# The last three output stores are issued from ScalarE's queue instead of SyncE's

## The chip, the cores and the metric

The kernel runs on one core of one Trainium2 chip. The metric is the device time of one execution in microseconds. Before the change it is 194.41 us, the median of three runs (194.31 to 195.1 us). One further execution was profiled; it took 194.51 us. Engines are named as the profile names them: PE is TensorE (PEld its weight loads), DVE is VectorE, ACT is ScalarE, POOL is GpSimd, SP is SyncE, which computes nothing and issues DMAs. A name with a q behind it (SPq, ACTq) is the sequencer of that engine, the part that takes the instructions in order, waits for semaphores and issues DMAs.

## The reference

A gated linear attention for 4 batches and 8 heads, followed by a block with a short causal convolution as a gate, and two matrix products:

```python
for t in range(S):                       # S = 768, per batch and head, D = 48
    state = f[:, :, t, :, None] * state + k[:, :, t] (x) v[:, :, t]
    y[:, :, t] = q[:, :, t] @ state
x = y as (B, S, 384)
gate = sigmoid(sum over 5 taps of conv_w[k] * x shifted by k)
out = (gate * (x @ w_val)) @ w_out
```

Here f is the sigmoid of f_logit, and (x) is an outer product.

## The kernel before

The 768 steps are cut into six chunks of 128. For each chunk the attention part makes the rows of x in SBUF, and the output part turns them into the result. The output part works on units: the tuples of UNITS say which chunk and which batches a unit holds. Chunks 1 to 4 are one unit each; the first and the last chunk are cut into two halves of two batches. The units of the last chunk are number 6 and number 7, and number 7 runs first. A unit has three column blocks of 128 (m or o is 0, 1, 2).

The order of all work is written out by hand in the string PROGRAM (line 54): every entry such as "mout 6 2" is a piece of the kernel with its unit and its block, and the loop on line 846 calls them in that order. The class Ordered ties each engine's instructions to the order in which they are recorded; since all are recorded through its one line, almost all instructions stand under line 129 in the profile, and one goes by the tiles' names.

For each block of a unit, "mout" runs nine matmuls on PE into a PSUM bank (bk), and "mstore" copies that bank into SBUF on ACT and then starts the DMA to the output from SP. Each DMA waits for the copy's semaphore. The program ends with:

```python
mout 7 2; mrest 6 1; mhigh 6 2; mmul 6 0; mrest 6 2; mhigh 6 0; mout 7 1; mstore 7 2; mrest 6 0; mout 6 2;
mstore 7 1; mout 6 1; mstore 6 2; mout 6 0; mstore 6 1; mstore 6 0
```

The six stores of the last chunk use six buffers in turn: ca, cb, ca, cb, osb, osb (four buffers that served the weights, and two that served earlier stores). In the order of the stores, the last three are block 2 of unit 6 out of the second cb, block 1 out of the first osb and block 0 out of the second osb. Each is 128 x 256 numbers, 128 KB. In store() (line 811), the list with the name ends counts these six.

DMAs use eight semaphores in turn. The store before the last three, the one of the second ca, has the first of them, the last three have the second, third and fourth.

Behind the last piece every engine does the same: it loads a flag (line 850, in the profile TENSOR_LOAD of bad) that says whether the inputs need a general path, and branches past that path (line 852, COMPARE_BRANCH). With these inputs all engines branch past it. On the far side each engine waits for its own unfinished work (line 852, EVENT_SEMAPHORE); SP has eight such waits, one for each DMA semaphore, in the order of the semaphores, so the last store is its fourth. Then SP has eight more on line 904 (the end of the program), and all engines meet in a closing barrier, also on line 904. SP loads the flag earlier than the others, ahead of its last twelve stores, so what it does behind its last DMA begins with the branch.

Of the kernel before, what the change touches and what calls it, by code (L numbers as in the profile page):

```python
# [140 lines left out]
def gla_moe(ctx: ExitStack, tc: tile.TileContext, q, k, f, v, wv, cw, wo, ft, out):  # L141
# [7 lines left out]
    PE, DVE, ACT, SP, POOL = (Ordered(tc, e) for e in (nc.tensor, nc.vector, nc.scalar, nc.sync, nc.gpsimd))  # L149
# [48 lines left out]
    def give(*key):  # L198
        free.append(held.pop(key))
# [359 lines left out]
    def mstart(xf, b0, b1, **t):  # L559
        return {"xf": xf, "b": slice(b0, b1), "n": (b1 - b0) * C, **t}  # L560
# [64 lines left out]
        w["po", o] = bank  # L625
        mm3(w["po", o][:, : w["n"]], lambda kk: woH[:, kk], lambda kk: woL[:, kk], w, "gH", "gL", o)

    def mstore(w, o, buf, dst):
        ACT.copy(buf, w["po", o][:, : w["n"]])
        SP.dma_start(dst, buf)  # L630

    def oview(c, o, b0=0, b1=B):
        return out[c, :, o, b0:b1].rearrange("p b t -> p (b t)")


    def general(ctx):
# [66 lines left out]
        with tc.For_i(0, NC, 1) as c:  # L703
            xf = gp.tile([128, NM, B, HALO + C], F32, name="gxf")
            for m in range(NM):
                for to, at, n in turned(m):
                    nc.sync.dma_start(xf[to : to + n, m], X[m * 128 + at : m * 128 + at + n, :, bass.ds(c * C, HALO + C)])
            w = mstart(xf, 0, B, **{n: gp.tile([128, NM, B, C], F32 if n == "gt" else F32R, name="g" + n)[:]
                                    for n in ("xH", "xL", "gt", "gH", "gL")})
            msplit(w)  # L710
            mlow(w)
            vps = [gb.tile([128, 1024], F32, name="vps") for _ in range(2)]
            for m in range(NM):
                w["gp", m] = vps[m // 2][:, m % 2 * 512 : m % 2 * 512 + 512]
            for j in range(KT):
                mconv(w, j)
            for m in range(NM):
                mgate(w, m)
            for m in range(NM):
                mval(w, m, gb.tile([128, 1024], F32, name="vps"))  # L720
                mmul(w, m)
                mhigh(w, m)
                mrest(w, m)
            for o in range(NM):
                mout(w, o, gb.tile([128, 1024], F32, name="vps"))
                mstore(w, o, g2.tile([128, B * C], F32, name="gosb")[:], out[bass.ds(c, 1), :, o].rearrange("u p b t -> (u p) (b t)"))
# [6 lines left out]
    proj, late, stored, ends = {}, {}, [], []  # L733

    def retag(tag, n, dtype=F32R):

        if tag not in late:
            late[tag] = mp.tile([128, n], dtype, name="r" + tag, tag=tag)
        return late[tag]

    def view(n):
        if n not in proj:
            c, b0, b1 = UNITS[n]
            at = (b0 // 2) * N2
            x = (dict(zip(("xH", "xL", "gt"), (t[:, :, b0:b1] for t in (xH, xL, gt)))) if c < last else

                 {"xH": part(retag("e2", 2 * N2), at, 2), "xL": part(retag(f"e1{(last - 2) % NE}", 2 * N2), at, 2)})
            proj[n] = mstart(XF[c % 2], b0, b1, turned=c >= CS, **x)
        return proj[n]
# [61 lines left out]
    def store(n, m):  # L811
        c, b0, b1 = UNITS[n]
        if c < last:
            buf = osb[len(stored) % len(osb)][:, : view(n)["n"]]
            stored.append(n)
        else:
            bufs = [t for ab in cab for t in ab] + osb
            buf = bufs[len(ends) % len(bufs)][:, : view(n)["n"]]
            ends.append(n)
        mstore(view(n), m, buf, oview(c, m, b0, b1))  # L820
        give("mout", n, m)

    def mul(n, m):
# [18 lines left out]
        "mval": lambda n, m: mval(view(n), m, take("mval", n, m)), "mmul": mul,  # L842
        "mhigh": lambda n, m: mhigh(gated(n), m), "mrest": lambda n, m: mrest(gated(n), m),
        "mout": lambda n, m: mout(gated(n), m, take("mout", n, m)), "mstore": store,
    }
    for piece in PROGRAM.replace("\n", " ").split(";"):
# [62 lines left out]
```

## Time and profile before

| what | value |
| --- | --- |
| median of three runs | 194.41 us |
| the profiled execution | 194.51 us |
| its span, from first to last instruction | 192.8 us |
| outside the span in that execution | 1.7 us |
| PE busy | 179.4 us (93%) |
| DVE busy | 161.4 us (84%) |
| ACT busy | 144.6 us (75%) |
| granted TensorE clock | 0.998 |
| DMAs issued by SP | all |

The first part of a page gives the busy time of each engine. DMA-issuing, waiting and branching instructions count as no engine's busy time, and so the chain of waits of the profile ends with the last computing instruction. What comes behind it is seen only in the rows of the sequencers (names with a q), which the views by line and by tile show. In the rows of a DMA issue, "us to landing" runs from the start of the issue to the arrival of the last of its sixteen semaphore increments.

### The profile page before, as it was taken

What the parts mean: (1) busy time and instruction counts of PE and PEld (TensorE: products, weight loads), DVE (VectorE), ACT (ScalarE), POOL (GpSimd) and SP (SyncE); (2) the same over time, 40 slices, a digit from 0 to 9 for tenths busy, and PEclk for the clock granted to TensorE, in tenths of its full rate; (3) what the DMA queues carried; (4) which work ended last, traced back from release to release, by engine and by line L of the source; (5) the groups of instructions that cost most, each with busy time, mean ns of one, the idle gap of its engine ahead of it and who ended that gap; (6) DMA issues with size and microseconds to landing.
All of it is one profiled execution on the core that took longest, in us unless ns stands there. A gap on an engine that the chain in (4) does not pass through costs nothing.

```text
span 192.8 us, 8306 instructions
## 1 busy us (share of the span) xinstructions
PE 179.4 (93%) x3706; PEld 144.3 (75%) x3706; DVE 161.4 (84%) x233; ACT 144.6 (75%) x284; POOL 16.0 (8%) x42
## 2 busy tenths in 40 slices
PE   3999999987999899999999999999999999999970
PEld 1888875675996468888788877878788778978960
DVE  7279899985998979979899998999993899998900
ACT  5899896999789997579999988594555856258530
POOL 6020111231000350000000000000000000000000
PEclk9999999999999999999999999999999999999999
DMA  5999999998647232643922319334000130011231
GB/s 199 331 411 423 418 415 405 409 346 248 191 124 297 15 112 55 212 142 113 341 79 84 112 53 313 84 137 167 3 3 3 58 111 3 3 58 54 86 113 39
DMA packets 12522, 32.64 MB, mean 169 GB/s; under 512 B 3008, under 2 KB 5440, under 8 KB 11456
## 3 DMA queue, kind: packets, MB, share of 16 engines
q1 hardware_dynamic: 12480, 32.04, 46.9%
q8 instruction: 31, 0.51, 1.1%
q14 instruction: 11, 0.09, 0.2%
HBM read 26.51 MB, written 4.72 MB: 162 GB/s over the span
## 4 chain that ended last, share of the span: by engine, by line
PE 59%; DVE 22%; ACT 9%; issue 5%; POOL 0%
PE bk L129 52%; PE aps L129 8%; DVE re L129 7%; DVE gt L129 5%; ACT ss L129 3%; DVE asb L129 2%; ACT xf L129 2%; DVE ca L129 1%; DVE cb L129 1%; DVE xL L129 1%; DVE kb L129 1%; ACT e L129 1%; DVE rg L129 1%; ACT gt L129 1%; DVE qb L129 1%
## 5 line engine op out<-in xcount | busy, mean ns | idle before, releaser
L129 ACT ACTIVATE e<-e 112x512 f32<-112x512 f32 (+4 forms) x38 | 36.7, 997 | 4.2 <-DMA e<-in_ft 2.0
L129 DVE TENSOR_TENSOR asb<-aps,tri 128x768 f32<-128x768 f32 (+1 forms) x24 | 25.0, 1040 | 7.0 <-PE aps L129 5.9
L129 PE MATMUL bk<-rg,woH 128*128 128x512 f32 (+1 forms) x108 | 30.1, 365 | 0.1
L129 DVE SCALAR_TENSOR_TENSOR gt<-xf,cws,gt 128x512 f32<-128x512 f32 x36 | 26.5, 749 | 1.5 <-ACT gt L129 0.9
L129 PEld LDWEIGHTS aps<-qb,kb 48*64 48x64 f32 (+1 forms) x640 | 19.9, 144 | 7.3 <-issue 4.8
L129 PE MATMUL bk<-asb,vb 128*32 128x64 f32 (+2 forms) x1280 | 24.2, 232 | 0.4 <-issue 0.3
L129 PE MATMUL aps<-qb,kb 48*64 48x128 f32 (+2 forms) x640 | 23.7, 257 | 0.1
L129 PEld LDWEIGHTS bk<-asb,vb 128*32 128x32 f32 (+1 forms) x1280 | 19.9, 108 | 4.0 <-issue 1.1
L129 PEld LDWEIGHTS bk<-rg,woH 128*128 128x128 f32 x108 | 18.6, 188 | 4.2 <-issue 0.8
L129 PE MATMUL bk<-rg,woL 128*128 128x512 f32 (+1 forms) x54 | 19.3, 358 | 0.0
L129 DVE TENSOR_TENSOR kb<-kb,e 112x1024 f32<-112x1024 f32 (+1 forms) x13 | 14.8, 1137 | 5.2 <-ACT e L129 5.0
L129 DVE TENSOR_TENSOR_SCAN e<-keep,e 112x1024 f32<-112x1024 bf16 x8 | 18.3, 2282 | 0.0
L129 ACT ACTIVATE ss<-u,e 112x48 f32<-112x48 f32 x64 | 15.3, 322 | 3.3 <-PE bk L129 3.3
L129 PE MATMUL bk<-qb,ss 48*32 48x128 f32 x640 | 15.8, 275 | 1.8 <-ACT cb L129 0.9
L129 ACT COPY osb<-bk 128x512 f32<-128x512 f32 (+1 forms) x20 | 9.8, 494 | 8.3 <-DMA out<-osb 5.1
L129 DVE TENSOR_TENSOR qb<-qb,e 112x1024 f32<-112x1024 f32 (+1 forms) x13 | 15.0, 1160 | 0.0
L129 ACT COPY xf<-bk 128x384 f32<-128x384 f32 x24 | 10.8, 471 | 5.2 <-PE bk L129 5.2
L129 PEld LDWEIGHTS bk<-qb,ss 48*32 48x32 f32 x640 | 10.6, 106 | 4.8 <-issue 3.1
L129 PE MATMUL bk<-xH,wvH 128*128 128x256 f32 (+1 forms) x36 | 13.3, 370 | 0.0
L129 PE MATMUL bk<-xL,wvH 128*128 128x256 f32 (+1 forms) x36 | 12.2, 339 | 0.0
L129 POOL MEMSET mark<- 1x1 f32 x18 | 1.6, 88 | 127.7 <-PE bk L129 127.7
L129 PE MATMUL bk<-xH,wvL 128*128 128x256 f32 (+1 forms) x36 | 12.2, 338 | 0.0
(107 smaller groups left out, 350.9 us busy)
## 6 DMA issues: line engine op xcount, KB each, us to landing
kb<-in_k SPq DMA_DIRECT2D x9, 512.0 KB, 4.5
qb<-in_q SPq DMA_DIRECT2D x9, 512.0 KB, 5.0
e<-in_f SPq DMA_DIRECT2D x4, 1024.0 KB, 10.3
vb<-in_v SPq DMA_DIRECT2D x9, 448.0 KB, 4.4
out<-osb SPq DMA_DIRECT2D x12, 256.0 KB, 2.1
raww<-in_wv SPq DMA_DIRECT2D x1, 1152.0 KB, 9.0
raww<-in_wo SPq DMA_DIRECT2D x1, 1152.0 KB, 11.3
kb<-in_k SPq DMA_DIRECT2D x1, 1024.0 KB, 13.6
```

Of the source, the lines that this page charges most:

```text
L129: ins = emit(*a, **kw)
```

## The change

The function mstore gets the queue that issues the DMA as an argument. store() passes ACT for the fourth to the sixth store of the last chunk, and SP for all others. The copies, buffers, transfers and their order stay.

```diff
-    def mstore(w, o, buf, dst):
+    def mstore(w, o, buf, dst, queue=SP):
         ACT.copy(buf, w["po", o][:, : w["n"]])
-        SP.dma_start(dst, buf)
+        queue.dma_start(dst, buf)
...
             ends.append(n)
-        mstore(view(n), m, buf, oview(c, m, b0, b1))
+
+        mstore(view(n), m, buf, oview(c, m, b0, b1), ACT if len(ends) > 3 else SP)
         give("mout", n, m)
```

One line is added to the file ahead of the end, so lines 850, 852 and 904 become 851, 853 and 905.

On ACT, at the end of the program, in one piece of the difference between the two programs (each row with the semaphores that it waits for; DMAHW are the eight DMA semaphores, PE_49, DVE_49 and Activation_49 those of the engines):

```order
 L129 COPY cb_104<-bk_110 128x256 [waits PE_49]
+L129 DMA out<-cb_104 128x256 [waits Activation_49]
 L129 COPY osb_97<-bk_106 128x256 [waits DMAHW4_49,PE_49]
+L129 DMA out<-osb_97 128x256 [waits Activation_49]
 L129 COPY osb_98<-bk_111 128x256 [waits DMAHW5_49,PE_49]
-L850 TENSOR_LOAD bad [waits DVE_49]
-L852 COMPARE_AND_BRANCH
+L129 DMA out<-osb_98 128x256 [waits Activation_49]
+L851 TENSOR_LOAD bad [waits DVE_49]
+L853 COMPARE_AND_BRANCH
```

Each of ACT's last three copies is now followed by a DMA that waits for that copy, and the flag and the branch come behind the third DMA.

On SP, at the same place:

```order
 L129 DMA out<-cb_102 128x256 [waits DMAHW7_49,Activation_49]
 L129 DMA out<-ca_103 128x256 [waits DMAHW0_49,Activation_49]
-L129 DMA out<-cb_104 128x256 [waits DMAHW1_49,Activation_49]
-L129 DMA out<-osb_97 128x256 [waits DMAHW2_49,Activation_49]
-L129 DMA out<-osb_98 128x256 [waits DMAHW3_49,Activation_49]
-L852 COMPARE_AND_BRANCH
+L853 COMPARE_AND_BRANCH
```

The branch follows directly on the store of ca_103 now. The eight waits behind SP's branch and the eight on the end line are the same in both programs.

## The prediction

> **What bounds the kernel now.** I read the chain of waits first, at its end, since the edit touches only the last stores. It closes like this (start, duration, what):
>
> ```profile
> 183.60 3.35 PE bk L129 x26
> 186.95 0.02 issue
> 186.97 0.37 ACT osb L129
> ```
>
> So PE paces the work up to 186.95 us, and the last computing instruction, the copy behind it, ends at 187.34. The span is 192.84. The windows view, which gives the busy time of PE, PEld, DVE, ACT and POOL, says what stands between the two:
>
> ```profile
> 187.40:192.84 5.44, 0.00 (x0) 0.00 (x0) 0.00 (x0) 0.00 (x0) 0.00 (x0) 0.94 0.15 45
> ```
>
> Nothing computes for 5.44 us. What ends last there is a sequencer. The timeline of the two queues shows the last three copies on ACT, and the last store on SP:
>
> ```profile
> 184.84 0.37 ACT L129 COPY cb<-bk 128x256 f32<-128x256 f32 x1 [1.07 <-PE bk L129]
> 185.91 0.37 ACT L129 COPY osb<-bk 128x256 f32<-128x256 f32 x1 [0.69 <-PE bk L129]
> 186.97 0.37 ACT L129 COPY osb<-bk 128x256 f32<-128x256 f32 x1 [0.69 <-PE bk L129]
> 183.81 0.39 SPq L129 DMA_DIRECT2D out<-ca  x1
> 185.24 0.33 SPq L129 DMA_DIRECT2D out<-cb  x1
> 187.37 0.82 SPq L129 DMA_DIRECT2D out<-osb  x1
> ```
>
> SP issues the last store 0.03 us behind the copy's end and is done with it at 188.19. Then the view of line 852 (the branch past the general path, and the waits behind it), engine by engine, with durations in ns and first and last start:
>
> ```profile
> L852 SPq EVENT_SEMAPHORE  x8: 17/17/17, 190.9 to 191.4; - x8
> L852 SPq COMPARE_BRANCH  x1: 45/45/45, 188.2 to 188.2; - x1
> L852 ACTq COMPARE_BRANCH  x1: 50/50/50, 187.6 to 187.6; - x1
> L852 ACTq EVENT_SEMAPHORE  x1: 17/17/17, 188.0 to 188.0; - x1
> L852 DVEq COMPARE_BRANCH  x1: 72/72/72, 183.7 to 183.7; - x1
> L852 DVEq EVENT_SEMAPHORE  x1: 21/21/21, 186.9 to 186.9; - x1
> L852 PEldq COMPARE_BRANCH  x1: 4138/4138/4138, 185.3 to 185.3; - x1
> L852 PEldq EVENT_SEMAPHORE  x1: 51/51/51, 189.5 to 189.5; - x1
> ```
>
> SP branches at 188.2 and its next instruction starts at 190.9. SP's list of waits books the same time as its own, not as a DMA's:
>
> ```profile
> SPq L852 <- SPq L852: 2.6, 1, 2.6
> ```
>
> DVE loses 3.1 us (183.8 to 186.9) and PE 4.1 us at the same branch, and neither issues DMAs; ACT loses 0.4. So I take SP's 2.6 us as the price of the jump itself, not as a wait for the store. The Trainium skill ("Runtime: NRT & Kernel Launch", section "Instruction fetch mechanics") has a name for it: a taken branch whose target lies outside the fetched window waits for a DMA of code.
>
> Is the store perhaps just as late? Landing times of the last five stores, in the order of issue (183.38, 183.81, 185.24, 186.31, 187.37), from the DMA view of short windows:
>
> ```profile
> out<-cb SPq DMA_DIRECT2D x1, 128.0 KB, 1.7
> out<-ca SPq DMA_DIRECT2D x1, 128.0 KB, 2.7
> out<-cb SPq DMA_DIRECT2D x1, 128.0 KB, 3.8
> out<-osb SPq DMA_DIRECT2D x1, 128.0 KB, 3.1
> out<-osb SPq DMA_DIRECT2D x1, 128.0 KB, 2.8
> ```
>
> The last store lands at 187.37 + 2.8 = 190.2. SP's wait for it is the fourth of its eight, which start evenly from 190.9 to 191.4, 0.07 us apart: at 191.1, about 0.9 us after the landing. **So the branch on SP, begun only behind the last store's issue, sets the end of the kernel; the store is second, 0.9 us behind.** From that fourth wait to the end of the span it is 192.84 - 191.1 = 1.7 us. This stretch holds SP's other four waits, the ones on line 904 and the closing barrier:
>
> ```profile
> L904 SPq EVENT_SEMAPHORE  x10: 17/28/28, 191.5 to 192.7; - x10
> L904 SPq DRAIN  x3: 7/7/7, 192.0 to 192.3; - x3
> ```
>
> SP reaches the barrier at 192.0; the others were there before (PE, the next, at about 189.6).
>
> **The change part by part.** *SP loses three issues.* Its last is now the store of ca, 183.81 + 0.39 = 184.2, and the branch follows. With its own 2.6 us SP is through at 186.8, with PE's 4.1 us at 188.3. Both lie ahead of the last landing, so SP's jump leaves the path, and its waits will stand ready for the last store. Nothing else queues on SP.
>
> *ACT gains three issues.* No row of this trace shows a DMA issued by ACT. The nearest are SP's:
>
> ```profile
> L129 SPq DMA_DIRECT2D out<-osb x20: 332/338/819, 77.5 to 187.4; - x20
> L129 SPq DMA_DIRECT2D wvLt<-wvL x4: 550/594/1390, 47.7 to 50.4; - x4
> ```
>
> Like transfers take 0.34 us as a rule and 0.82 at most; no SP issue of another shape takes over 1.39. I take SP's own values at the same three places, 0.33, 0.33 and 0.82. Queued behind the first two issues are ACT's next copies, each of which waits 0.69 us for PE before it starts; behind the first copy's end (185.21) and the second's start (185.91) there is room for an issue of some 0.6 us. So they cost nothing, hidden under PE's nine matmuls per block; beyond 0.6 us each further 0.1 us is paid twice. PE and DVE wait for no instruction behind these issues. The third store then starts at 187.37, as before.
>
> Behind the third issue ACT still has to load the flag, which stood under its last copy before:
>
> ```profile
> L850 ACTq TENSOR_LOAD <-bad x1: 562/562/562, 187.0 to 187.0; - x1
> ```
>
> That gives 188.2 + 0.56 + 0.05 for the branch + 0.4 for its jump = 189.2, ahead of the landing, and level with PE's 189.5. It costs nothing as long as ACT's jump stays short; if it took SP's 2.6, ACT would be at the barrier at 191.5.
>
> *What is late next: the landing of the third store.* The end of the span becomes landing + 1.7. Bounds for issue to landing are the rows above, 1.7 and 3.8 us: landing from 189.1 to 191.2. By its own row, 2.8, it is 190.2. Between issue and landing SP's code fetch runs in the program of before. Packets of code in two windows of the DMA view, 186.2:186.5 and 189.2:189.4 (packets, MB, share of 16 engines in the window):
>
> ```profile
> q8 instruction: 1, 0.02, 33.4%
> q14 instruction: 1, 0.01, 10.7%
> ```
>
> These are 0.334 x 16 x 0.3 = 1.6 us and 0.107 x 16 x 0.2 = 0.34 us on a DMA engine that stores use too. The first falls in PE's jump, and the stores issued nearest to it (185.24, 186.31) are the ones with the longest landings. The second comes 1.0 us after SP's branch, ahead of the last landing; it moves to about 185.2. An estimate: of its 0.34 us half is saved, so I take the landing at 190.0, between 190.2 and 189.8.
>
> **The sum.** 190.0 + 1.7 = 191.7 for the span, against 192.84: 1.1 us less. The profiled execution would go from 194.51 to 193.4; it stood 0.1 us above the median of the runs, so the forecast is **193.3 us**.
>
> Here a rule weighs in. The Trainium skill ("DMA: Bandwidth & Descriptors", section "Issuing engines are not separate DMA queues") says that issuing from several engines saves no more than sequencer time, since all transfers run on the same 16 engines. Where the trace bears on it, it agrees: the code packets and the stores share engines. By that rule the landing would stay at 190.2 and the sum at 0.9 us less, 193.5.
>
> **The rivals.** *The landing slips (193.6 to 194.4).* SP's code packet, and what it fetches ahead, now run at 185 to 188, beside PE's packet of 1.6 us, when the three stores are in flight. If the last share of the third store lands 0.1 to 0.9 us later than 190.2, only 0.8 to 0 us is left. For it speaks the 3.8 row of the cb store; against it, that the store in question is issued last, at 187.37. ACT's jump at 2.6 us would end alike: 191.5 + 0.8 from SP's 192.0 to the span's end = 192.3, 194.0. It decides from a landing of 190.2, or an arrival of ACT at the barrier after 191.0.
>
> *The third issue's stall goes (192.4).* The 0.82 is 0.48 above the usual. If on ACT's queue it takes 0.34 and lands like the first cb store, in 1.7, the landing is 189.1, the end 190.8, 2.0 us less. For it: a queue of its own with only two stores ahead. Against it: the PE code packet stays where it is.
>
> *A dear issue on ACT (slower, 195.6).* At 1.39 us per issue: first 185.24 to 186.63, copy until about 187.06, second until 188.5, copy until 188.9, third until 190.3. From the end of an issue to the landing it took 2.8 - 0.82 = 2.0 us in the last store: landing 192.3, end 194.0, 1.2 us more. It loses from about 1.0 us per issue; for less the jump's gain covers it. Against it: the median of 338 ns over the twenty osb stores.
>
> *The change does not do what it says:* the order of the instructions shows SP's branch right behind ca, so this is out unless SP's jump also takes until 190.9, 6.7 us; the longest is 4.1.
>
> **How the numbers follow.** About 0.5%, 1.0 us, is what a measurement of this kernel can tell from no change. Forecast case 0.45, 0.03 of it under that line; stall gone 0.15, faster; landing slips or ACT's jump grows 0.33, the same; dear issue 0.07, 0.05 of it slower. That makes faster 0.57, same 0.38, slower 0.05. The bounds of the landing, 189.1 to 191.2, make 192.4 to 194.5; I leave out a thin edge below: 192.5 to 194.5.
>
> **What would show it.** Right: SP's branch on line 853 at 184.2, its first wait after it no later than 188.3, three waits there passing at once and the fourth standing until the landing near 190.0; ACT's issues at 185.24, 186.31 and 187.37, its copies not moved; the closing barrier 1.7 us after the landing. Wrong: ACT issues over 0.6 us, copies that start late, ACT or PE at the barrier behind SP, or a fourth wait that ends past 190.2.

## The result, and the profile after

The changed kernel takes 193.37 us (median of 22 runs, 192.74 to 194.68) against 194.41 us for the kernel before in 22 runs beside it. The ratio is 0.9946 with a 95% interval of 0.9926 to 0.9965: about 1.05 us, 0.5%, faster. Slow executions of a kernel (over 1.5% above its fastest) are left out of this ratio and of those below, and of the profiles only that of the run "held" below is of such a one. The profiled execution took 193.15 us, with a span of 191.5 us in place of 192.8.

The chain of waits of the kernel after ends just as before (start, duration, what):

```profile
183.58 3.35 PE bk L129 x26
186.93 0.02 issue
186.96 0.37 ACT osb L129
```

In these two profiled executions the last copy ends within 0.01 us of the same moment, 187.33 after and 187.34 before. So nothing was won up to there, and the difference lies behind it. The windows view of the kernel after, from the end of the last copy to the end of the span, and below it the same stretch of the kernel before:

```profile
187.33:191.48 4.15, 0.00 (x0) 0.00 (x0) 0.00 (x0) 0.00 (x0) 0.00 (x0) 0.78 0.21 62
187.34:192.84 5.50, 0.00 (x0) 0.00 (x0) 0.00 (x0) 0.00 (x1) 0.00 (x0) 0.94 0.16 48
```

4.15 us without a computing instruction, against 5.50 before: 1.35 us less. Below, this stretch is called the end. The timeline of the kernel after shows the three issues, now on ACT's queue:

```profile
185.23 0.38 ACTq L129 DMA_DIRECT2D out<-cb  x1
186.30 0.34 ACTq L129 DMA_DIRECT2D out<-osb  x1
187.36 0.56 ACTq L129 DMA_DIRECT2D out<-osb  x1
```

They start where SP's started (185.24, 186.31, 187.37), so ACT's copies behind them were not pushed back. What follows on the sequencers, from the view of line 853 (line 852 before; durations in ns, first and last start in us):

```profile
L853 SPq COMPARE_BRANCH  x1: 45/45/45, 184.2 to 184.2; - x1
L853 SPq EVENT_SEMAPHORE  x8: 17/17/17, 187.5 to 190.1; - x8
L853 ACTq COMPARE_BRANCH  x1: 54/54/54, 188.5 to 188.5; - x1
L853 ACTq EVENT_SEMAPHORE  x1: 17/17/17, 188.7 to 188.7; - x1
L853 PEldq EVENT_SEMAPHORE  x1: 51/51/51, 189.3 to 189.3; - x1
```

SP branches at 184.2 and reaches its first wait at 187.5. Its eight waits, which took 0.5 us before, now stretch over 2.6: they stand there until the stores land. From the DMA view of the kernel after, in three short windows at the starts of the issues (us to landing last):

```profile
out<-cb ACTq DMA_DIRECT2D x1, 128.0 KB, 3.7
out<-osb ACTq DMA_DIRECT2D x1, 128.0 KB, 3.0
out<-osb ACTq DMA_DIRECT2D x1, 128.0 KB, 2.4
```

The last lands at 187.36 + 2.4 = 189.8. The same view of line 853 for SP alone, in the window from 189.5:

```profile
L853 SPq EVENT_SEMAPHORE  x5: 17/17/17, 189.8 to 190.1; - x5
```

The fourth wait, the first of these five, starts as the last store lands, and from there it is 1.7 us to the end, as before. SP's jump still costs what it did, and more; its list of waits books the sum of what SP spent behind its branch, with the longest piece last:

```profile
SPq L853 <- SPq L853: 5.5, 4, 3.2
```

3.2 us against 2.6. Only its place has changed: it runs from 184.3 to 187.5, beside PE's last matmuls and ACT's last copies.

### The profile page after: what moved, and what is told of

Its sections match the earlier page's. It is cut to its first block, busy times and chain, and to the rows that moved or that the text cites. A ratio compares the mean times of both kernels' runs of the same rounds, so it can differ in the third digit from the quotient of the medians.

```text
span 191.5 us, 8303 instructions
## 1 busy us (share of the span) xinstructions
PE 180.2 (94%) x3706; PEld 144.8 (76%) x3706; DVE 162.2 (85%) x233; ACT 144.8 (76%) x284; POOL 13.7 (7%) x42
## 4 chain that ended last, share of the span: by engine, by line
PE 56%; DVE 19%; ACT 13%; issue 6%; DMA 3%; POOL 0%; ACTq 0%; DVEq 0%
PE bk L129 49%; PE aps L129 8%; DVE re L129 7%; DVE gt L129 5%; ACT ss L129 4%; DMA out<-osb 3%; ACT e L129 2%; ACT xf L129 2%; DVE asb L129 2%; DVE qb L129 1%; DVE rg L129 1%; DVE xL L129 1%; ACT osb L129 1%; DVE rqb L129 1%; ACT re L129 1%
## 5 line engine op out<-in xcount | busy, mean ns | idle before, releaser
L129 ACT CAST rg<-gt 128x512 fp32r<-128x512 f32 (+1 forms) x18 | 9.3, 546 | 3.7 <-DVE gt L129 3.7
```

Source lines behind the costliest of these rows:

```text
L129: ins = emit(*a, **kw)
```

## The experiments

The first question is what the gain hangs on. Theory 1: on SP's jump, which left the end of the path. Theory 2: on the queue, a store being better off when ACT issues it. Since a single profiled execution can reach its last copy a microsecond or two earlier or later than another of a nearly equal kernel (186.84 to 189.00 in the kernels of this section whose general path is whole), the ends are compared in the profiles, and the totals by their ratios to the kernel before, run beside each.

**Two on ACT, the last one on SP.**

```diff
-        mstore(view(n), m, buf, oview(c, m, b0, b1), ACT if len(ends) > 3 else SP)
+        mstore(view(n), m, buf, oview(c, m, b0, b1), ACT if len(ends) in (4, 5) else SP)
```

> Only the fourth and fifth of the last six stores go to ACT; the very last one stays on SP, so SP's branch again begins behind its issue, at about 188.2 us. Theory 1 (the gain is SP's jump past the general path, taken out of the end of the path): SP's first wait on line 853 again at about 190.9, span 192.8, time as before, ratio 0.998 to 1.002. Theory 2 (a store gains by being issued from ACT's own queue, each of the three its share): two thirds of the gain, a ratio near 0.9965, span 192.0.

Ratio 0.9986 (0.9959 to 1.0013), which can't be told from no change. The timeline of SP's queue, the view of its line 853, and the window of the end:

```profile
186.87 0.33 SPq L129 DMA_DIRECT2D out<-osb  x1
```

```profile
L853 SPq COMPARE_BRANCH  x1: 45/45/45, 187.2 to 187.2; - x1
L853 SPq EVENT_SEMAPHORE  x8: 17/17/17, 189.9 to 190.4; - x8
```

```profile
186.84:191.87 5.03, 0.00 (x0) 0.00 (x0) 0.00 (x0) 0.00 (x1) 0.00 (x0) 0.86 0.18 52
```

With SP's branch back behind the last issue, its eight waits again follow each other at 0.07 us, so the jump and not the store sets the end. The end is 5.03 us: 0.88 us worse than the change, which is what theory 1 asks. But it is also 0.47 us better than the kernel before, which theory 1 did not expect, and the row of the issue says where from: 0.33 us in place of 0.82. So theory 2 has a part of its own. With its two predecessors on the other queue, SP's last issue runs through, and the branch comes that much earlier.

**Only the very last store on ACT.**

```diff
-        mstore(view(n), m, buf, oview(c, m, b0, b1), ACT if len(ends) > 3 else SP)
+        mstore(view(n), m, buf, oview(c, m, b0, b1), ACT if len(ends) > 5 else SP)
```

> Only the very last store goes to ACT. Theory 1: SP's last issue ends at about 186.7, its jump of 2.6 to 3.2 us ends at 189.3 to 189.9, at or ahead of the last landing near 189.8, so nearly the whole gain stays: span 191.4 to 191.8, ratio 0.994 to 0.997. Theory 2: one third of the gain, span 192.4, ratio near 0.998.

Ratio 0.9955 (0.9920 to 0.9989). Line 853 on SP, and the end:

```profile
L853 SPq COMPARE_BRANCH  x1: 45/45/45, 187.8 to 187.8; - x1
L853 SPq EVENT_SEMAPHORE  x8: 17/17/17, 190.8 to 191.3; - x8
```

```profile
188.44:192.72 4.28, 0.00 (x0) 0.00 (x0) 0.00 (x0) 0.00 (x0) 0.00 (x0) 1.00 0.21 61
```

One store moved gives 1.22 of the 1.35 us. SP's branch begins 0.6 us ahead of the last copy's end, at 188.44, and that is nearly enough: the jump and the landing (188.47 + 2.5 = 191.0) end together. Theory 2's third of the gain is not what the end shows; the interval of the total holds both theories.

**All three on ACT, but SP's branch held back.** A tiny load on SP, behind its last store, waits for the last copy; and as a control the same load without that wait. The list copies collects the copies of mstore; that part and the making of the tile tiny are left out here.

```diff
...
+    tail = SP.dma_start(tiny, q[0, :, 0, 0:16])
+    tc.add_manual_dep(tail.ins, copies[-1].ins.name, SYNC, reason="the last copy is through")
```

> The changed kernel, and on SP behind its last store one tiny load (128 x 16 numbers) that waits for the last copy, so that SP's branch begins at 187.7 to 188.2 as in the kernel before, while all three stores are issued by ACT. Theory 1: the gain is gone: SP's first wait on line 860 at 190.4 to 191.4, span 192.3 to 193.3, ratio 0.998 to 1.003. Theory 2: the gain stays, span 191.5, ratio 0.995.

> The control of the run before: the same tiny load on SP, but without the wait for the last copy, so SP issues it at about 184.2 and branches at 184.6. Both theories: as the changed kernel, ratio 0.9945 give or take 0.002, span 191.4 to 191.6. If it is slower, the tiny load itself costs, and the run before is read against this one.

Held: ratio 0.9993 (0.9963 to 1.0022). Of its profile only the end is read here. The timeline, line 860 (the branch in this kernel), and the end:

```profile
189.03 0.34 SPq L129 DMA_DIRECT2D tiny<-in_q  x1
189.03 0.91 ACTq L129 DMA_DIRECT2D out<-osb  x1
```

```profile
L860 SPq COMPARE_BRANCH  x1: 45/45/45, 189.4 to 189.4; - x1
L860 SPq EVENT_SEMAPHORE  x8: 17/17/17, 192.2 to 192.7; - x8
```

```profile
189.00:194.14 5.14, 0.00 (x0) 0.00 (x0) 0.00 (x0) 0.00 (x1) 0.00 (x0) 0.84 0.19 55
```

The control: ratio 0.9963 (0.9929 to 0.9998), with its line 856 (the branch in this kernel) and its end:

```profile
L856 SPq EVENT_SEMAPHORE  x8: 17/17/17, 187.3 to 189.9; - x8
L856 SPq COMPARE_BRANCH  x1: 45/45/45, 184.5 to 184.5; - x1
```

```profile
187.12:191.36 4.24, 0.00 (x0) 0.00 (x0) 0.00 (x0) 0.00 (x1) 0.00 (x0) 1.00 0.20 61
```

Same stores, same queue, same extra load; the branch begun late costs 0.9 us of the end (5.14 against 4.24), and the total can't be told from the kernel before. This is theory 1 by itself. The intervals of the two ratios overlap, so it rests on the profiles' ends. The pieces of this end are those of the other profiles: from SP's first wait to the end of the span it is 1.96 us, as in the kernel before and in the run with two on ACT, and the jump of 2.7 us lies between their 2.6 and the control's 2.8.

**The long jump taken away.** The body of the general path is cut to one memset and eight small DMAs, in the kernel before and in the changed one. With these inputs the path is not run, so no work of these executions is left out; only the code that the branch passes over is shorter. The new body, the function short, is left out here.

```diff
...
-        general(sub)
+        short(sub)
```

> The kernel before, with the body of the general path cut to one memset and eight small DMAs (with these inputs it is not run), so that the target of every engine's branch stands a few instructions on; the eight waits of SP behind the branch stay. Theory 1 (SP's jump over the general path sets the end): the jump on SP drops from 2.6 us to that of ACT, some 0.4 us or less, PE's and DVE's too, and with PE's code packet gone the last store lands 1.7 to 2.0 us after its issue. From the end of the last copy to the end of the span 3.5 to 3.9 us in place of 5.5, ratio 0.990 to 0.993. Theory 2 (stores are better off on ACT's queue): the stores on SP stay late, and this kernel keeps about 1 us behind the next run.

> The changed kernel with the same cut of the general path. Theory 1: no gain is left to the change, since there is no long jump to take off the path: within 0.2 us of the run before, 3.5 to 3.9 us from the end of the last copy to the end of the span, ratio 0.990 to 0.993. Theory 2: about 1 us faster than the run before it.

Line 861 (the branch) of the cut kernel before, its landings from the DMA view of the window 184 to 192, and its end:

```profile
L861 SPq COMPARE_BRANCH  x1: 50/50/50, 188.9 to 188.9; - x1
L861 SPq EVENT_SEMAPHORE  x8: 17/17/17, 189.1 to 190.6; - x8
L861 PEldq COMPARE_BRANCH  x1: 223/223/223, 186.4 to 186.4; - x1
```

```profile
out<-cb SPq DMA_DIRECT2D x2, 128.0 KB, 1.7
out<-osb SPq DMA_DIRECT2D x2, 128.0 KB, 1.7
out<-ca SPq DMA_DIRECT2D x1, 128.0 KB, 1.8
```

```profile
188.53:191.97 3.44, 0.00 (x0) 0.00 (x0) 0.00 (x0) 0.00 (x1) 0.00 (x0) 0.84 0.18 60
```

And the end of the cut changed kernel:

```profile
190.84:194.28 3.44, 0.00 (x0) 0.00 (x0) 0.00 (x0) 0.00 (x1) 0.00 (x0) 1.00 0.19 63
```

The two ends are equal to 0.01 us. Where the jump is short (SP branches at 188.9 and stands at its first wait at 189.1), it makes no difference to the end which queue issues the stores. Both ends are 2.06 us shorter than that of the kernel before, and each of the last five stores lands 1.7 or 1.8 us after its issue, where the last four took 2.7 to 3.8 with the long jump. So the cut takes three things away at once: the jump, the late landings and the long third issue.

The totals did not follow: 1.0004 (0.9966 to 1.0041) and 1.0017 (0.9982 to 1.0052). The ends being 2 us shorter, the way up to the last copy must be about 2 us longer. The cut had also shrunk a DRAM scratch tensor of the general path, so a second pair kept that at its old size.

> The first cut kernels had the expected end (3.44 us behind the last copy in both) but a longer way up to the last copy. They had also shrunk the DRAM scratch tensor of the general path, which shifts other addresses. Here the code of the general path is cut as before, and the scratch tensor keeps its size. The end must again be 3.4 to 3.5 us. If the scratch tensor was the reason for the longer way, the last copy ends at 186.5 to 188.0 us again and the ratio is 0.988 to 0.992. If the shorter code was, the last copy ends at 188.5 or later on average and the ratio is 0.998 to 1.003.

> The same for the changed kernel. End 3.4 to 3.5 us, as in the run before it, since with a short jump the choice of queue is worth nothing: the two runs within 0.3% of each other. Ratio 0.988 to 0.992 if the scratch tensor was the reason for the longer way, 0.998 to 1.003 if the shorter code was.

Ratios 0.9952 (0.9916 to 0.9988) and 0.9965 (0.9933 to 0.9998), and the ends of the one and of the other:

```profile
188.71:192.13 3.42, 0.00 (x0) 0.00 (x0) 0.00 (x0) 0.00 (x0) 0.00 (x0) 1.00 0.18 61
```

```profile
188.38:191.83 3.45, 0.00 (x0) 0.00 (x0) 0.00 (x0) 0.00 (x0) 0.00 (x0) 1.00 0.19 62
```

The ends are as expected once more, and again equal. The ratios lie between the two that were to tell the reasons apart: more than 1 us of the 2 stays lost ahead of the last copy. Neither reason is shown, and why a shorter program behind the branch makes a longer way ahead of it stays open. It also means that no kernel here beats the changed one by shortening the general path.

**The stalled third issue.** First and third store on ACT, second on SP.

```diff
-        mstore(view(n), m, buf, oview(c, m, b0, b1), ACT if len(ends) > 3 else SP)
+        mstore(view(n), m, buf, oview(c, m, b0, b1), ACT if len(ends) in (4, 6) else SP)
```

> Of the last three stores the first and the third go to ACT, the second to SP, so that no queue holds two unfinished stores when the third is issued. If the long third issue (0.82 us on SP before, 0.56 on ACT after) comes from two unfinished stores on its own queue, all three issues take 0.33 to 0.40 here. SP's branch begins at 186.7, and its jump ends at 189.3 to 189.9. If the last landing is set by the shares that stand behind code packets on one DMA engine, it stays 2.3 to 2.6 us after the issue, span 191.4 to 191.7, ratio as the changed kernel, 0.993 to 0.997. If the landing follows the issue's length, it comes some 0.2 us earlier, span 191.2.

Ratio 0.9955 (0.9923 to 0.9987). Timeline of the three issues, and the end:

```profile
186.30 0.38 ACTq L129 DMA_DIRECT2D out<-cb  x1
187.36 0.33 SPq L129 DMA_DIRECT2D out<-osb  x1
188.42 0.34 ACTq L129 DMA_DIRECT2D out<-osb  x1
```

```profile
188.39:192.58 4.19, 0.00 (x0) 0.00 (x0) 0.00 (x0) 0.00 (x1) 0.00 (x0) 0.97 0.20 63
```

```profile
L853 SPq EVENT_SEMAPHORE  x8: 17/17/17, 190.6 to 191.2; - x8
L853 SPq COMPARE_BRANCH  x1: 45/45/45, 187.7 to 187.7; - x1
```

No issue stalls, as expected. Together with the other runs: the third store took 0.82, 0.56, 0.91, 0.69 and 0.66 us (before, after, held, control, and the run below) where its own queue had issued the two before it, and 0.33 to 0.38 where at most one of them was on its queue and unlanded. In the cut kernels three on one queue took 0.33 to 0.34.

The traces say when a stall ends. With the long path a code packet of 16 KB (q8 instruction) starts 0.9 us behind PE's branch in every profile, and in the cut kernels none does, so it is taken as PE's. In the kernel after it stands in the window 186.2:186.5 like this:

```profile
q8 instruction: 1, 0.02, 27.7%
```

That is 0.277 x 16 x 0.3 = 1.33 us, from 186.22 to 187.55; in the kernel before it took 1.60 us, from 186.20 to 187.80. The stalled issues end at 187.92 and 188.19, 0.37 and 0.39 us behind the packet, and in the other three stalled runs 0.37 to 0.47 us behind it. In the run of this section, with the second store on SP, the packet ended only 0.04 us after the third issue began, so it could hardly show a stall. The runs with two and with one on ACT do: there the packet ran on for 0.5 us after the third issue began, and the issue took 0.33 and 0.38 us. Two unlanded stores ahead on the queue are not enough by themselves: in the kernel before and in the run with one on ACT the second store (186.31 and 187.40) had two, under PE's packet, and took 0.33 us. So a stall goes with PE's packet and with the queue's two earlier stores; what exactly holds the issue is not shown.

The end is no shorter for it, 4.19: here the last store lands 2.0 us after its issue, at 190.4, but SP's jump, begun at 187.7, ends only at 190.6.

**The last store's place among the waits.** Four tiny loads earlier in the program turn the semaphores on by four, so that the last store is SP's eighth wait and not its fourth.

```diff
...
     def check():
+        for i in range(4):
+            SP.dma_start(tiny[:, 16 * i : 16 * i + 16], q[0, :, 0, 0:16])
```

> The changed kernel with four tiny loads (128 x 16 numbers each) on SP ahead of the last chunk, which turn the semaphores on by four, so that the last store has the eighth of SP's eight waits behind the branch and not the fourth. If the waits behind the landing are on the path one by one, 0.07 us each, the end comes 4 x 0.07 = 0.28 us earlier: 1.42 us from the landing to the end of the span in place of 1.70, span about 191.2, ratio near 0.993. If they are not, 1.70 stays. The rival theory of the store's queue has nothing to say here.

Ratio 0.9948 (0.9917 to 0.9979). Line 856 on SP (its waits in this kernel) in the window from 190.5, and the end:

```profile
L856 SPq EVENT_SEMAPHORE  x1: 17/17/17, 190.7 to 190.7; - x1
```

```profile
188.18:192.09 3.91, 0.00 (x0) 0.00 (x0) 0.00 (x0) 0.00 (x1) 0.00 (x0) 1.00 0.22 62
```

From the last wait to the end it is 192.09 - 190.7 = 1.4 us, 0.3 less, and the end is 0.24 us shorter than that of the changed kernel. The waits behind the landing are on the path one by one. In the total 0.24 us is 0.12%, which these runs can't tell from nothing.

## Why the prediction was right

*The bound.* SP's branch behind the last issue was named as what sets the end, with the landing 0.9 us behind it. That holds: the branch held back costs 0.9 us of the end, and with a short jump the choice of queue is worth nothing.

*SP's three issues gone.* SP was to branch at 184.2 and be through between 186.8 and 188.3. It branched at 184.2 and was through at 187.5.

*ACT's three issues.* 0.33, 0.33 and 0.82 us were taken over from SP. They took 0.38, 0.34 and 0.56, the first two hidden under PE's matmuls as said; the rival of a dear issue falls. The rival by which the third issue's stall goes came true in part, with 0.56 us between 0.82 and 0.34. ACT's flag and jump ended at 188.7, ahead of the landing.

*The landing.* Taken as 190.0, measured 189.8, so the rival of a slipped landing falls. The size was about right; the reason given is not shown. SP's code packet did move to 185.2, but in the run with two on ACT SP's jump still came behind the last issue, and the store landed after 2.5 us. What the traces show is that the first of a store's sixteen increments comes 1.2 us after the end of its issue (1.18 to 1.30 in the last five stores of all twelve kernels), so a stall puts off the landing. The last store landed 188.19 + 1.95 = 190.14 before and 187.92 + 1.85 = 189.77 after: 0.27 of the 0.37 us are the shorter third issue, and this goes with PE's code packet being 0.27 us shorter in the profile after. The prediction kept the 0.82 us of the issue, and no reason for a shorter packet is known; it was 1.2 to 1.7 us long in the eight profiles with the long path. That the landing came out near the forecast is in part luck.

*The rest to the end.* 1.7 us from the fourth wait on, as measured before and after.

*The sum.* 1.1 us was forecast for the span and 1.35 measured. The difference is the landing, 2.6 us from issue in the forecast and 2.4 measured, and in it the third issue. Seen from SP there are two parts in it: 0.47 us because the third issue no longer stalls on SP, which the run with two on ACT has without the rest, and 0.88 us for the jump. In the total the gain is 1.05 us, 0.7 to 1.4 by its interval. That it meets the forecast to 0.1 us is closer than either the working or the measurement allows.

*What was to show it.* One detail was wrong: three of SP's waits were to pass at once. Only the first did; the second and third stood for the landings of their own stores, 185.23 + 3.7 = 188.9 and 186.30 + 3.0 = 189.3. The prediction's own rows had these landings at 3.8 and 3.1 us, behind the end of SP's jump. This costs nothing, since the fourth is later.

*The rule of the Trainium skill* ("DMA: Bandwidth & Descriptors", section "Issuing engines are not separate DMA queues"), by which 0.9 us were to be expected, agrees with the traces in what it says of the transfers: with short jumps all stores land in 1.7 to 1.8 us from either queue. What it counts as saved is the time of the issue on its sequencer; here 1.35 us came off the end, since a jump queued behind the issue was on the path too.

## What to carry to other kernels

The chain of waits ends with the last computing instruction; what the sequencers do behind it (branches, waits, the closing barrier) was 5.5 us here, and the views of their lines show who is last. Where a program ends in a branch, let the engine that is last at the barrier reach it early, and leave the last DMAs to one whose branch is short or that is idle anyway: one moved store did nearly all of it. A cut at the very end of a kernel can be read from two profiles to about 0.1 us, as the stretch behind the last copy (3.42 to 3.45 us in the four cut kernels, 4.15 and 4.24 in the changed kernel and the control), where the totals of single executions differ by more than a microsecond.

## What the runs showed of the hardware

The price of the same branch differs by engine: with the long path 2.6 to 3.2 us on SP, 2.9 to 3.6 on DVE, 3.6 to 4.4 on PE and 0.1 to 0.4 on ACT; with the short one 0.1 to 0.4 us on all four. The last three stores of 128 KB land 2.0 to 4.1 us after their issue with the long path and 1.7 to 1.8 with the short one. With the long path the first two of them have fifteen of their sixteen increments within 1.1 us of each other and the last one 0.6 to 2.4 us later; with the short path it comes within 0.04 us. The third one, behind two others of its queue, takes 0.56 to 0.91 us to issue and not 0.34, on SP and on ACT alike, and its issue ends 0.37 to 0.47 us behind PE's code packet. That PE's code packet holds them up on a DMA engine that it shares with them fits all of this, but was not tried apart from the jumps. An issue of these stores that does not stall takes 0.34 to 0.38 us on ACT, against 0.33 on SP.
